# Two token tiles of the first MLP's second slice group computed together by seven block products

## The chip, the cores and the metric

The kernel runs on one core of one Trainium2 chip. The metric is the time of one execution on the device in microseconds (us); the kernel before has a median of 665.19 us over three runs (664.45, 665.19, 665.57).

## The reference

Three layers follow each other, all in float32. The first is a decaying linear attention over 2 batches, 8 heads and 768 positions with 64 channels. Its output becomes 1536 tokens of 512 channels. The second (MoE 1 in the code) and the third (MoE 2) are gated MLPs:

```python
# attention, per 64-position block (the kernel uses 128-position chunks)
intra = (q @ k.T * Dmask) @ v
inter = (q * lam_pow) @ kv_state
kv_state = lam_block * kv_state + (k * rev_pow).T @ v

# MoE 1: 1536 tokens, d_model 512, d_ff 1536
xn = x / sqrt(mean(x * x, -1) + 1e-6) * rms_g
g = xn @ w_gate
x = (g * sigmoid(g) * (xn @ w_val)) @ w_out

# MoE 2: the same shapes, no norm
out = ((x @ w_a) * (x @ w_b)) @ w_out
```

## The kernel before, in words

**Precision.** TensorE multiplies operands that are split into a high and a low part, and a product of two split matrices takes three matmuls: high by high, high by low, low by high. ScalarE makes the high part by a copy into a shorter format (`hi`, `uh`, line 292), VectorE subtracts it to get the low part (`lo`, `ul`, line 297). Weights come from memory as 64-bit numbers: ScalarE takes them apart in two copies (word `c`, lines 245 and 249), and VectorE puts a float32 together in seven operations (`k`, lines 266 to 280).

**Tiling.** The 1536 tokens are three tiles of 512 (0, 1, 2). The 1536 hidden columns are 12 slices of 128, in two groups (0 to 5, 6 to 11), and a slice's weights are three pieces of 128x512: gate, value, output. One *step* is one slice for one tile: 12 matmuls of 512 columns into a gate bank (`G`), 12 into a value bank (`V`), ScalarE's silu (`si`), VectorE's product with the value (`mu`), the split of the result (`hh`, `hl`), and 12 matmuls with the output weights into the four accumulator banks acc0 to acc3 (`O`). After a group the accumulators are copied or added into `sums` (`E`). Each tile splits the weights anew.

**Pairs.** In MoE 2 tiles 1 and 2 go together, by a scheme of seven block products in place of eight. The two tiles, each cut in two along the contraction, are the four blocks of one operand (B11, B21, B12, B22), gate and value of a slice those of the other. VectorE forms four sums of weight blocks (`ws`), the blocks' differences T1 to T4 are made once (`td`, `th`, `tl`), and seven products of 6 matmuls (`P`) go to three banks, with ScalarE's snapshots between them (`ps`) and VectorE's sums (`pa`). A product, a split and output matmuls follow as in a step (`pm`, `ph`, `pl`, `Q`). Since there are only four accumulator banks, tile 2's output matmuls wait until tile 1's are summed.

**Order.** Nothing is scheduled by a rule: the string PROGRAM lists every operation as a word (`G.12` is the gate of step 12), and each engine executes its words in that order. The queues of the engines are in order; a word waits for the data, buffers and PSUM banks that it needs. In MoE 1 before, steps run slice group by slice group, tile by tile: steps 18 to 23 are slices 6 to 11 for tile 0, 24 to 29 for tile 1, 30 to 35 for tile 2. Step 12 is the first after attention has ended.

**Norm.** For chunk c and batch b, ScalarE squares the attention output (`sq`), VectorE adds four column blocks in one reduction (`rd`, line 424), TensorE adds over partitions by a matmul with ones (`R`), VectorE adds epsilon (`ms`), GpSimd takes the power (`rr`), VectorE builds a diagonal (`dg`), TensorE spreads it (`N`), and VectorE scales four blocks (`nx`) before the split (`xh`, `xl`). `W` words are bf16 matmuls whose result nobody reads.

**Homes.** A converted weight slice lives in one of 8 slots of 128x1536; `third_of` puts the output piece of slice i into the slot of slice i+1.

Of the kernel before, what the change touches and what calls it, by code (L numbers as in the profile page):

```python
# [7 lines left out]
F32 = mybir.dt.float32  # L8
# [32 lines left out]
SLOTS = 8  # L41
# [7 lines left out]
    A.0.0.0 W.14 W.7.1 S.0.0 A.0.0.2 l.0 g Z A.1.0.0 A.1.0.2 D.0 A.0.1.0 D.1 l.1 A.1.1.3 A.1.1.0 A.1.1.2 c.0.1  # L49
    S.1.0 A.0.1.2 l.2 A.0.1.3 k.0.0.1 k.0.4.1 k.0.2.1 k.0.1.1 k.0.3.1 k.0.5.1 am.0.0.0 k.0.6.1 am.0.0.1 am.1.0.1  # L50
    am.1.0.0 kd.0.0 kd.1.0 X.0.0 U.0.0 hi.0.0 sq.0.0 xg.0.0 X.1.0 U.1.0 lo.0.0 l.3 L.0.2 sa.0.0 rd.0.0 sa.1.0
    qd.0.1 I.0.1 S.0.1 sq.1.0 c.0.2 xg.1.0 c.1.0 rd.1.0 am.0.1.1 S.1.1 am.0.1.0 k.0.0.2 k.0.4.2 am.1.1.0 R.0 ms.0
    am.1.1.1 qd.1.1 X.0.1 sq.0.1 l.4 W.8.1 I.1.1 X.1.1 sd.0.1 k.0.1.2 k.0.3.2 k.0.2.2 k.0.5.2 kd.1.1 rr.0 dg.0
    k.0.6.2 l.5 N.0 U.1.1 c.1.1 hi.0.1 xg.0.1 L.1.2 rd.0.1 sd.1.1 kd.0.1 nx.0.1 nx.0.3 nx.0.0 sq.1.1 lo.0.1 sa.1.1
    rd.1.1 nx.0.2 qd.0.2 U.0.1 xh.0.0 c.1.2 xh.0.1 xg.1.1 kd.0.2 R.1 ms.1 rr.1 xl.0.0 sa.0.1 k.1.0 xl.0.1 k.1.1
    dg.1 k.1.4 N.1 nx.1.3 nx.1.0 nx.1.1 nx.1.2 c.2.0 xh.1.0 k.1.3 xl.1.0 xh.1.1 k.1.5 xl.1.1 k.1.2 S.0.2 am.0.2.1
    am.0.2.0 l.9 l.7 l.6 kd.1.2 qd.1.2 c.2.2 c.2.1 G.0 l.8 I.0.2 X.0.2 U.0.2 si.0 sq.0.2 xg.0.2 L.0.3 sd.0.2 l.10
    k.2.0 k.1.6 rd.0.2 k.2.4 k.2.2 k.2.1 sa.0.2 k.2.3 V.0 hi.1.0 hi.0.2 c.3.0 hi.1.1 c.3.2 c.3.1 S.1.2 lo.1.0
    k.2.5 am.1.2.0 lo.0.2 mu.0 G.1 am.1.2.1 l.11 qd.0.3 U.1.2 I.1.2 X.1.2 sd.1.2 kd.0.3 l.13 l.12 k.3.0 lo.1.1
    k.2.6 hh.0 si.1 sq.1.2 rd.1.2 hi.2.0 sa.1.2 lo.2.0 k.3.2 k.3.1 k.3.4 k.3.3 V.1 R.2 ms.2 c.4.2 hi.1.2 hl.0 O.0  # L60
# [743 lines left out]
```

## Time and profile before

| | |
|---|---|
| median of 3 runs | 665.19 us |
| the profiled execution | 664.28 us, of which the span of its instructions 662.6 us |
| TensorE at work | 97% of the span |
| VectorE at work | 74% |
| ScalarE at work | 59% |
| GpSimd at work | 6% |
| mean granted TensorE clock | 0.987 |
| read from memory | 51.1 MB |

Times inside the span count from its first instruction. "Busy" counts a stretch in which several instructions overlap once. TensorE's instructions overlap (the next starts before the one ahead has ended), so a matmul's length in a row is not what it costs in a sequence; the distance from one start to the next is. The chain of work that ended last cuts such overlaps off, so its pieces add up.

### The profile page before, as it was taken

The numbers are of one execution on the slowest core, as the hardware profiler recorded it, in microseconds if no ns is written. First come the engines' busy times: TensorE is split into PE (matmuls) and PEld (weight loads), VectorE is DVE, ScalarE is ACT, GpSimd is POOL, SyncE is SP. The second block draws the span as 40 slices with busy tenths as digits, with TensorE's granted clock in tenths as the row PEclk, the third lists the DMA queues.
The fourth block names the chain that finished last, engine by engine and source line by source line (L and its number), as shares of the span: only waits on it lengthen the run. The fifth ranks groups of instructions, "written<-read, shape, count | busy, mean of one in ns | idle before, by whom it ended". The sixth has DMA issues, their size and how long they took to land.

```text
span 662.6 us, 8558 instructions
## 1 busy us (share of the span) xinstructions
PE 640.3 (97%) x3300; PEld 520.4 (79%) x3301; DVE 490.0 (74%) x781; ACT 389.1 (59%) x610; POOL 42.2 (6%) x43
## 2 busy tenths in 40 slices
PE   6869999999999999999999999999999999999997
PEld 4657787777888888888888888888887888888876
DVE  4789999865663878567357999887784797766583
ACT  2758777333578684364387974755648953444431
POOL 2523231210000000000000000000000000000000
PEclk9969999999999999999999999999999999999999
DMA  8946454110033331030033430201102400100011
GB/s 273 377 129 226 153 193 160 64 64 1 1 96 124 100 101 58 1 95 1 1 125 124 127 101 1 95 1 63 33 0 69 154 1 1 63 1 0 1 63 64
DMA packets 16505, 54.83 MB, mean 83 GB/s; under 512 B 1864, under 2 KB 3408, under 8 KB 15440
## 3 DMA queue, kind: packets, MB, share of 16 engines
q1 hardware_dynamic: 15600, 47.99, 22.0%
q10 hardware_dynamic: 864, 6.29, 2.7%
q8 instruction: 26, 0.43, 0.3%
q14 instruction: 15, 0.12, 0.1%
HBM read 51.12 MB, written 3.15 MB: 82 GB/s over the span
## 4 chain that ended last, share of the span: by engine, by line
PE 89%; DVE 8%; DMA 1%; issue 1%; ACT 0%; POOL 0%; DVEq 0%; POOLq 0%; ACTq 0%; SPq 0%
PE acc L534 29%; PE at L645 10%; PE gv L486 8%; PE gv L645 7%; PE gv L490 7%; PE gv L487 7%; PE at L490 5%; PE at L486 5%; PE at L487 5%; PE at L338 1%; PE at L388 1%; PE at L373 1%; DVE nrm L445 1%; DVE wlo L297 1%; DVE sums L546 1%; PE acc L388 1%
## 5 line engine op out<-in xcount | busy, mean ns | idle before, releaser
L297 DVE TENSOR_TENSOR wlo<-w,whi 128x512 fp32r<-128x512 f32 (+1 forms) x192 | 124.1, 674 | 10.2 <-ACT whi L292 10.0
L292 ACT CAST whi<-w 128x512 fp32r<-128x512 f32 (+1 forms) x192 | 108.9, 607 | 13.4 <-DVE w L278 7.0
L486 PE MATMUL gv<-xhi,whi 128*128 128x512 f32 x240 | 96.5, 402 | 0.3 <-DVE s L505 0.3
L487 PE MATMUL gv<-xlo,whi 128*128 128x512 f32 x240 | 94.4, 393 | 0.0
L245 ACT COPY hh<-stage 128x1024 uint8<-128x1024 uint8 x72 | 75.2, 1044 | 8.6 <-DMA stage<-w_dram 6.8
L509 ACT CAST hhi<-s 128x512 fp32r<-128x512 f32 x48 | 29.8, 621 | 78.9 <-DVE s L505 78.9
L249 ACT COPY w<-stage 128x1024 uint16<-128x1024 uint16 x72 | 75.4, 1047 | 0.0
L490 PE MATMUL gv<-xhi,wlo 128*128 128x512 f32 x240 | 64.5, 390 | 1.1 <-DVE wlo L297 1.0
L513 DVE TENSOR_TENSOR hlo<-s,hhi 128x512 fp32r<-128x512 f32 x48 | 34.6, 721 | 30.5 <-ACT hhi L509 30.4
L486 PE MATMUL at<-xhi,whi 128*128 128x512 f32 x144 | 56.0, 389 | 0.0
L487 PE MATMUL at<-xlo,whi 128*128 128x512 f32 x144 | 56.0, 389 | 0.0
L486 PEld LDWEIGHTS gv<-xhi,whi 128*128 128x128 f32 x240 | 45.6, 190 | 11.5 <-issue 0.9
L490 PEld LDWEIGHTS gv<-xhi,wlo 128*128 128x128 f32 x240 | 44.9, 188 | 11.3 <-DVE wlo L297 1.9
L487 PEld LDWEIGHTS gv<-xlo,whi 128*128 128x128 f32 x240 | 45.7, 190 | 9.1
L534 PE MATMUL acc<-whi,hlo 128*128 128x512 f32 x144 | 43.0, 391 | 0.0
L278 DVE SCALAR_TENSOR_TENSOR w<-w,hh 128x1536 f32<-128x1536 uint32 (+1 forms) x26 | 42.4, 1630 | 0.4
L534 PE MATMUL acc<-hhi,whi 128*128 128x512 f32 x144 | 42.1, 394 | 0.4 <-ACT hhi L509 0.4
L534 PE MATMUL acc<-hlo,whi 128*128 128x512 f32 x144 | 41.7, 391 | 0.9 <-DVE hlo L513 0.9
L534 PE MATMUL acc<-whi,hhi 128*128 128x512 f32 x144 | 42.2, 392 | 0.1
L534 PE MATMUL acc<-wlo,hhi 128*128 128x512 f32 x144 | 41.8, 389 | 0.0
L534 PE MATMUL acc<-hhi,wlo 128*128 128x512 f32 x144 | 41.5, 389 | 0.0
L505 DVE TENSOR_TENSOR s<-s,gv 128x512 f32<-128x512 f32 x30 | 20.5, 683 | 27.3 <-PE gv L490 27.2
(144 smaller groups left out, 1138.7 us busy)
## 6 DMA issues: line engine op xcount, KB each, us to landing
stage<-w_dram SPq DMA_DIRECT2D x72, 512.0 KB, 3.5
att<-att_dram ACTq DMA_DIRECT2D x6, 1024.0 KB, 4.8
att<-att_dram SPq DMA_DIRECT2D x6, 512.0 KB, 5.9
out_dram<-sums SPq DMA_DIRECT2D x12, 256.0 KB, 2.1
att<-att_dram SPq DMA_DIRECT2D x2, 1024.0 KB
att<-att_dram SPq DMA_DIRECT2D x4, 256.0 KB, 7.9
dt<-ext_d SPq DMA_DIRECT2D x2, 256.0 KB, 4.7
p<-ext_d SPq DMA_DIRECT2D x2, 128.0 KB, 6.3
```

The lines of the kernel that those rows point to most:

```text
L245: nc.scalar.copy(hh_t[i][:, into].bitcast(U8).rearrange("p (n e) -> p n e", e=2), st.rearrange("p (n e) -> p n e", e=8)[:, :, 3:5],)
L249: nc.scalar.copy(wres[i][:, into].bitcast(U16).rearrange("p (n e) -> p n e", e=2), st.bitcast(U16).rearrange("p (n e) -> p n e", e=4)[:, : ...
L278: nc.vector.scalar_tensor_tensor(out=w, in0=w32, scalar=2.0**-28, in1=hh.bitcast(BF16), op0=ALU.mult, op1=ALU.mult)
L292: nc.scalar.copy(whi[key], src)
L297: nc.vector.tensor_sub(wlo[key], src, whi[key].bitcast(F32))
L486: nc.tensor.matmul(ps, lhsT=w, rhs=xhi[t][:, k, :], start=k == 0, stop=False)
L487: nc.tensor.matmul(ps, lhsT=w, rhs=xlo[t][:, k, :], start=False, stop=False)
L490: nc.tensor.matmul(ps, lhsT=w, rhs=xhi[t][:, k, :], start=False, stop=k == KD - 1)
L509: nc.scalar.copy(h_t[g][0], s_t[g])
L513: nc.vector.tensor_sub(h_t[g][1], s_t[g], h_t[g][0].bitcast(F32))
L534: nc.tensor.matmul(acc[j], lhsT=lhsT, rhs=rhs, start=first and n == 0, stop=last and n == 2)
L645: nc.tensor.matmul(ps, lhsT=w[:, k * 128 : (k + 1) * 128], rhs=x[:, k, :], start=first and n == 0, stop=n == len(todo) - 1, skip_group_che ...
```

## The change

In MoE 1, slices 6 to 11 are computed for tiles 1 and 2 together by the seven block products that MoE 2 had already. Steps 18 to 23 (tile 0) stay; steps 24 to 35 of before go, and six paired slices take their place. For these, the blocks' differences are formed from the high and low parts that lie in SBUF (`tq`), and then split (`tH`, `tL`); ScalarE's silu is applied to the finished gate (`sl`).

Output pieces get homes of their own: 7 slots of 128x1024 for gate and value, 10 of 128x512 for output pieces. Two of the seven conversion operations (numbers 2 and 6) become two instructions each, one for each home.

In the norm of chunks 0 and 1 the reduction on VectorE goes: four matmuls add the squares' four blocks up in PSUM. Mean and epsilon go by batch. PROGRAM is written anew from start to end, with 46 matmuls of `W` in place of 29.

```diff
-SLOTS = 8
+SLOTS, OUT_SLOTS = 7, 10
...
-    A.0.0.0 W.14 W.7.1 S.0.0 A.0.0.2 l.0 g Z A.1.0.0 A.1.0.2 D.0 A.0.1.0 D.1 l.1 A.1.1.3 A.1.1.0 A.1.1.2 c.0.1
+    A.0.0.0 W.8.1 W.14 W.3.1 W.7.1 W.2.1 S.0.0 W.3.1 A.0.0.2 l.0 g Z A.1.0.0 A.1.0.2 D.0 D.1 A.0.1.0 A.1.1.3
...
+    def home(i, some):
+        if some.start == 0:
+            if i - 1 not in wout:
+                wout[i - 1] = wpool.tile([128, 512], F32, tag=f"o{(i - 1) % OUT_SLOTS}", name=f"o{i - 1}")
+            return wout[i - 1]
+        if i not in wres:
+            wres[i] = wpool.tile([128, 1024], F32, tag=f"w{i % SLOTS}", name=f"w{i}")
+        return wres[i][:, (some.start - 1) * 512 : (some.stop - 1) * 512]
...
+        if op in (2, 6):
+            for some in (slice(0, 1), slice(1, 3)) if place is None else (slice(place, place + 1),):
+                w = home(i, some)
+                hh = hh_t[i][:, some.start * 512 : some.stop * 512]
...
-    def mean_square(c):
-        ms_t[c] = ps = bank("at0")
-        for b in range(B):
-            nc.tensor.matmul(ps[:, b : b + 1], lhsT=sqs_t[b, c], rhs=ones[:, 0:1], start=True, stop=True)
+    def mean_square(b, c):
+        ms_t[b, c] = att_bank(b, c)
+        todo = [sqs_t[b, c]] if (b, c) in sqs_t else [sq_t[b, c][:, a * C : (a + 1) * C] for a in range(NP)]
+        for n, x in enumerate(todo):
+            nc.tensor.matmul(
+                ms_t[b, c][:, 0:1], lhsT=x, rhs=ones[:, 0:1], start=n == 0, stop=n == len(todo) - 1
+            )
...
-        for m in range(2) for lo, hi in GROUPS for t in range(1 if m else len(TILES)) for f in range(lo, hi)
+        for m in range(2) for lo, hi in GROUPS for t in range(1 if m or lo else len(TILES)) for f in range(lo, hi)
...
+    DIFFS = {
+        3: (("B12h", "B11h"), ("B12l", 1), ("B11l", -1)), 4: (("B22h", "T1"), ("B22l", 1)),
+        5: (("B22h", "B12h"), ("B22l", 1), ("B12l", -1)), 6: (("B21h", "T2"), ("B21l", 1)),
+    }
...
+    def part_diff(n, s):
...
+        if s == 0:
+            nc.vector.tensor_sub(o, of(a), of(b))
+        elif b == 1:
+            nc.vector.tensor_add(o, o, of(a))
+        else:
+            nc.vector.tensor_sub(o, o, of(a))
+
+    def diff_hi(n, k):
+        nc.scalar.copy(block(BLOCKS[n])[0][:, k, :], diff_home(n)[:, k, :])
+
+    def diff_lo(n, k):
+        hi, lo = block(BLOCKS[n])
+        nc.vector.tensor_sub(lo[:, k, :], diff_home(n)[:, k, :], hi[:, k, :].bitcast(F32))
...
+    def pair_silu(i, t):
+        nc.scalar.activation(s_t[i, t], s_t[i, t], AF.Silu)
```

Three places show how the instructions move. Lines 486, 487, 490 and 534 of before are 514, 515, 518 and 562 now.

TensorE, MoE 1, slice 6 for tile 1, before: the gate bank gv0 is filled by 12 matmuls from tile 1's parts (xhi1, xlo1), then the value bank.

```order
L486 MATMUL gv0_2522<-xhi1_778,whi_2482 128x512
L487 MATMUL gv0_2522<-xlo1_779,whi_2482 128x512
L486 MATMUL gv0_2522<-xhi1_778,whi_2482 128x512
L487 MATMUL gv0_2522<-xlo1_779,whi_2482 128x512
L490 MATMUL gv0_2522<-xhi1_778,wlo_2484 128x512 x4
L486 MATMUL gv1_2559<-xhi1_778,whi_2486 128x512
```

The same engine now, at slice 6 for tiles 1 and 2, from the end of tile 0's last output matmuls on: products 7, 4 and 3 of the slice (T3 is a difference block, xhi2 and xlo2 hold tile 2 or a difference).

```order
L562 MATMUL acc3_2405<-hlo_2622,whi_2588 128x512
L706 MATMUL gv0_2636<-T3_2489,whi_2643 128x512 x4
L706 MATMUL gv0_2636<-T3_2489,wlo_2645 128x512 x2
L706 MATMUL gv0_2636<-xhi2_1480,whi_2656 128x512
L706 MATMUL gv0_2636<-xlo2_1481,whi_2656 128x512
L706 MATMUL gv0_2636<-xhi2_1480,whi_2656 128x512
L706 MATMUL gv0_2636<-xlo2_1481,whi_2656 128x512
L706 MATMUL gv0_2636<-xhi2_1480,wlo_2662 128x512 x2
L706 MATMUL at0_2664<-xhi2_1480,whi_2643 128x512
```

Products of 6 matmuls stand where steps of 36 stood, and product 4 follows product 7 into the same bank with nothing between; ScalarE's snapshot of product 7 has to read that bank first.

VectorE in the paired slices now, around slices 9 and 10 (wsum are sums of weight blocks, h2 and s are gates and products of tiles 2 and 1, o12 and w13 are homes of MoE 2's weights).

```order
L727 TENSOR_TENSOR h2_2802<-h2_2802,usum_2351 128x512
L675 TENSOR_TENSOR wsum_2221<-w9_1973 128x256
L675 TENSOR_TENSOR wsum_2221<-w9_1973,wsum_2221 128x256
L301 TENSOR_TENSOR hh_2710<-hh_2710,t_2824 128x1536
L727 TENSOR_TENSOR s_2819<-s_2819,gv1_2840 128x512
L317 TENSOR_TENSOR wlo_2903<-o8_1980,whi_2891 128x512
L286 SCALAR_TENSOR_TENSOR o12_2760<-o12_2760,hh_2710 128x512
L286 SCALAR_TENSOR_TENSOR w13_2712<-w13_2712,hh_2710 128x1024
L317 TENSOR_TENSOR wlo_2931<-w9_1973,whi_2900 128x512
```

Sums, splits and pair products of MoE 1 and the conversion of MoE 2's weights (lines 301 and 286) share the queue; before, tile 1's and tile 2's steps stood there.

VectorE in the norm of the first chunk, before (line 424 is the reduction, am a masked score, wlo a weight's low part).

```order
L349 TENSOR_TENSOR am<-gv_176,dt 128x512
L297 TENSOR_TENSOR wlo<-w_172,whi 128x512
L424 TENSOR_REDUCE nrm<-sq 128x128 x2
L349 TENSOR_TENSOR am<-at_268,dt 128x512
L349 TENSOR_TENSOR am<-at_267,dt 128x512
L266 TENSOR_SCALAR t<-hh 128x512
```

The same place now (line 461 adds epsilon, for one batch; lines 349, 297 and 266 are 369, 317 and 293 now).

```order
L369 TENSOR_TENSOR am<-gv_200,dt 128x512
L286 SCALAR_TENSOR_TENSOR w_197<-w_197,hh 128x512
L461 TENSOR_SCALAR ms<-acc_282 128x1
L369 TENSOR_TENSOR am<-at_258,dt 128x512
L369 TENSOR_TENSOR am<-at_259,dt 128x512
L317 TENSOR_TENSOR wlo<-w_197,whi 128x512
L293 TENSOR_SCALAR t<-hh 128x512
```

The two reductions are gone from this place, two more from a later one, and the epsilon of batch 0, which waits for TensorE, stands ahead of the next chunk's masks.

## Rows read from the trace of the kernel before

**Rows 1.** The page: span, busy time and share by engine.

```profile
span 662.6 us, 8558 instructions
PE 640.3 (97%) x3300; PEld 520.4 (79%) x3301; DVE 490.0 (74%) x781; ACT 389.1 (59%) x610; POOL 42.2 (6%) x43
```

**Rows 2.** Busy time by stretch: length, then each engine's, clock, DMA share, GB/s.

```profile
0.00:42.50 42.50, 28.48 (x285) 20.97 (x286) 28.91 (x64) 22.40 (x32) 16.56 (x23) 0.83 0.80 279
42.50:113.40 70.90, 67.72 (x477) 53.29 (x476) 67.23 (x98) 54.11 (x77) 17.99 (x14) 0.98 0.53 179
278.60:376.50 97.90, 97.90 (x434) 81.09 (x433) 64.55 (x98) 63.47 (x96) 0.00 (x0) 1.00 0.23 72
376.50:425.60 49.10, 49.10 (x218) 40.69 (x217) 46.54 (x70) 32.98 (x52) 0.00 (x0) 1.00 0.22 73
425.60:518.10 92.50, 92.50 (x404) 75.35 (x404) 70.25 (x118) 59.25 (x100) 0.00 (x0) 1.00 0.14 43
```

**Rows 3.** The chain that ended last, by time: start, length, what; steps, then pairs.

```profile
243.36 2.72 PE acc L534 x12
251.52 2.72 PE acc L534 x12
...
458.94 1.36 PE gv L645 x6
460.30 0.68 PE acc L534 x3
460.98 1.65 PE gv L645 x6
```

**Rows 4.** VectorE's groups by form: count, busy us, mean ns, idle before and releasers.

```profile
L297 DVE TENSOR_TENSOR wlo<-w,whi 128x512 fp32r<-128x512 f32 x180 | 119.3, 691 | 10.2 <-ACT whi L292 10.0
L278 DVE SCALAR_TENSOR_TENSOR w<-w,hh 128x1536 f32<-128x1536 uint32 x23 | 40.3, 1753 | 0.4
L278 DVE SCALAR_TENSOR_TENSOR w<-w,hh 128x512 f32<-128x512 uint32 x3 | 2.1, 686 | 0.0
L424 DVE TENSOR_REDUCE nrm<-sq 128x128 f32<-128x512 f32 x12 | 12.9, 1078 | 9.9 <-ACT sq L420 9.9
L276 DVE TENSOR_TENSOR hh<-hh,t 128x1536 uint16<-128x1536 uint16 x23 | 22.0, 955 | 0.4
L268 DVE TENSOR_SCALAR t<-t 128x1536 uint16<-128x1536 uint16 x23 | 13.8, 602 | 0.4
L614 DVE TENSOR_TENSOR wsum<-wsum,w 128x256 f32<-128x256 f32 x12 | 5.1, 424 | 0.3
L604 DVE TENSOR_TENSOR sums<-sums,sums 128x1024 f32<-128x1024 f32 x3 | 3.7, 1218 | 0.0
```

**Rows 5.** VectorE's instructions in order of time, at 35, 42 and 400 us.

```profile
35.45 1.61 DVE L268 TENSOR_SCALAR t<-t 128x1536 uint16<-128x1536 uint16 x1
42.22 0.69 DVE L470 TENSOR_TENSOR xlo<-spare,xhi 128x512 fp32r<-128x512 f32 x1
399.77 1.89 DVE L297 TENSOR_TENSOR wlo<-w,whi 128x512 fp32r<-128x512 f32 x3
```

**Rows 6.** GpSimd's instruction beside the slow one of VectorE at 35 us.

```profile
34.94 1.71 POOL L329 TENSOR_TENSOR spare<-att,p 128x512 f32<-128x512 f32 x1
```

**Rows 7.** The chain at the first step's gate.

```profile
42.55 0.72 PE gv L486
43.27 0.43 PE gv L487
...
46.85 1.02 PE at L373 x16
47.87 1.05 PE at L388 x16
```

More of the change, by code (lines that the diff above doesn't have):

```diff
@@ L162 @@
+    uh.19.5 ul.19.5 ph.19.2 pl.19.2 Q.18.2.0.12 ph.20.2 uh.20.5 ul.20.5 pl.20.2 Q.19.2.0.12 uh.22.5 uh.21.5
+    ul.21.5 ph.21.2 pl.21.2 Q.20.2.0.12 ul.22.5 ph.22.2 pl.22.2 Q.21.2.0.12 uh.23.5 ul.23.5 ph.23.2 pl.23.2
+    Q.22.2.0.12 Q.23.2.0.12 e.23.2.0 e.23.2.1 e.23.2.2 e.23.2.3
 """.split()
@@ L228, in load_w @@
         stage[n] = t
-    wres, hh_t, t_t = {}, {}, {}
-    def third_of(i, part):
-        return (i + 1, 0) if part == 2 else (i, part + 1)
+    wres, wout, hh_t, t_t = {}, {}, {}, {}
+    def home(i, some):
[6 more added lines that the diff above has]
+        return wres[i][:, (some.start - 1) * 512 : (some.stop - 1) * 512]
     def conv_copy(i, place):
-        if i not in wres:
-            wres[i] = wpool.tile([128, 1536], F32, tag=f"w{i % SLOTS}", name=f"w{i}")
+        if i not in hh_t:
             hh_t[i] = vpool.tile([128, 1536], U16, tag="hh", name="hh")
@@ L249, in conv_copy @@
         nc.scalar.copy(
-            wres[i][:, into].bitcast(U16).rearrange("p (n e) -> p n e", e=2),
+            home(i, slice(place, place + 1)).bitcast(U16).rearrange("p (n e) -> p n e", e=2),
             st.bitcast(U16).rearrange("p (n e) -> p n e", e=4)[:, :, 0:2],
@@ L258, in conv_op @@
             place = 0
-        some = slice(0, 1536) if place is None else slice(place * 512, (place + 1) * 512)
         if i not in t_t and op != 2:
             t_t[i] = vpool.tile([128, 1536], U16, tag="t", name="t", bufs=1)
-        hh, w = hh_t[i][:, some], wres[i][:, some]
-        t = t_t[i][:, some] if op != 2 else None
-        w32 = w.bitcast(U32)
+        if op in (2, 6):
+            for some in (slice(0, 1), slice(1, 3)) if place is None else (slice(place, place + 1),):
+                w = home(i, some)
+                hh = hh_t[i][:, some.start * 512 : some.stop * 512]
+                w32 = w.bitcast(U32)
+                if op == 2:
+                    nc.vector.tensor_scalar(
+                        w32, w32, 0x0FFFFFFF, 0x10000000, op0=ALU.bitwise_and, op1=ALU.bitwise_or
+                    )
+                else:
+                    nc.vector.scalar_tensor_tensor(
+                        out=w, in0=w32, scalar=2.0**-28, in1=hh.bitcast(BF16), op0=ALU.mult, op1=ALU.mult
+                    )
+            return
+        some = slice(0, 1536) if place is None else slice(place * 512, (place + 1) * 512)
+        hh, t = hh_t[i][:, some], t_t[i][:, some]
         if op == 0:
@@ L274, in conv_op @@
             nc.vector.tensor_scalar(hh, hh, 0x8000, None, op0=ALU.bitwise_and)
-        elif op == 5:
+        else:
             nc.vector.tensor_tensor(out=hh, in0=hh, in1=t, op=ALU.bitwise_or)
-        else:
-            nc.vector.scalar_tensor_tensor(
-                out=w, in0=w32, scalar=2.0**-28, in1=hh.bitcast(BF16), op0=ALU.mult, op1=ALU.mult
-            )
     whi, wlo = {}, {}
     def third(i, part):
-        i, place = third_of(i, part)
-        return wres[i][:, place * 512 : (place + 1) * 512]
+        return wout[i] if part == 2 else wres[i][:, part * 512 : (part + 1) * 512]
     def unit_hi(key, src):
```

255 lines of the change are left out of this document (138 added, 117 removed).

## The prediction

> **What bounds the kernel now.** The page comes first: TensorE is at work for 97% of the span, VectorE for 74% [rows 1]. A mean over stages says little, so the stretches come next [rows 2]. From 278.6 to 518.1 us TensorE is busy every microsecond at the full clock; VectorE's share goes from 66% (64.55 of 97.90, plain steps) over 95% (46.54 of 49.10, where MoE 2's tile differences are made) to 76% (70.25 of 92.50, MoE 2's pairs). From 42.5 to 113.4 us it is the other way round: VectorE fills 67.23 of 70.90 us, and TensorE has gaps. The chain of waits gives the price of TensorE's work: output matmuls start at 243.36 and again at 251.52 us, so a step of 36 matmuls takes 8.16 us, 0.227 each, with nothing waited for [rows 3]. A matmul removed after step 12 is worth 0.227 us, as long as VectorE and ScalarE keep up.
>
> **Products: −8.16 us.** A slice for tiles 1 and 2 took two steps of 36 matmuls; it takes 7 products of 6 and 24 output matmuls, 66. Six slices drop 36 matmuls: 36 × 0.227 = 8.16 us.
>
> A rule speaks against that price. The Trainium skill ("Perfetto Trace Analysis", Identifying the Most-Contended Engine) says that matmul busy time shows badly how near TensorE is to its limit, and that the busy share of weight loads shows it better. That share is 79% here [rows 1]; an estimate by the rule would count 36 × 0.227 × 0.79 = 6.5 us. The distance of 0.227 us from start to start over a stretch without a wait speaks for the full price.
>
> **VectorE in the paired slices: +2 us, between 0 and 21.** What an instruction costs in a queue is the distance between starts: three splits of 0.69 us took 1.89 together [rows 5], so each costs 0.60, or 0.08 to 0.09 less than its length. Between the first product of slice 6 and step 24, VectorE's queue holds 96 sums, splits and products of the paired slices: 70 of 512 columns at 0.60 and 26 of 256 at 0.42 − 0.08 = 0.34 [rows 4], 51 us. It holds the conversion of five slices of MoE 2. Each has four 16-bit operations at 0.60 − 0.08, one at 0.95 − 0.08 [rows 4], a third operation at some 0.95, and the seventh, now in two parts of 0.69 and, half way to the 1.75 of 1536 columns, 1.22 [rows 4], less 0.17: 5.6 us, for five slices 28. And it holds 21 sums and splits of neighbouring stages at 0.60, 13 us. Together 92 us, where TensorE has 6 × 66 + 12 matmuls, 92.5 us. So VectorE has nothing to spare, and each gap of its queue that the conversions don't fill is TensorE's. The nearest rows: at 376.5 to 425.6 VectorE was 95% busy and TensorE waited for nothing, which is the lower end, 0. In MoE 2's six paired slices VectorE lay idle for 92.50 − 70.25 = 22.25 us [rows 2]; all of that beside 92 us of work would take 114 us, 21 more than TensorE's work. I take 2, one of them for one place: in slice 6 product 4 follows product 7 into the same bank. In MoE 2, where 3 matmuls (0.68 us) stood between such two, product 4 took 1.65 us in place of 6 × 0.227 = 1.36 [rows 3], so ScalarE's snapshot and its signals need 0.68 + 0.29 = 0.97 us, which nothing hides now. For the rest I stay near the lower end, 1 us: a low part is needed only by the last 2 of a product's 6 matmuls and the last 4 of the 12 of a gate or an output, and conversions can fill waits here as they did at 376.5.
>
> **Differences, homes: 0, between 0 and 4.** In steps 12 to 23 VectorE gets 12 × 5 instructions at 0.60 (36), six slices' conversions (34), ten differences of 1024 columns at 1.22 − 0.08 [rows 4] and eight splits (16): 86 us, where TensorE has 97.9. The steps at 278.6 show no gap at 66% of VectorE, the row after it none at 95% [rows 2]; this is 88%. Were the differences not covered by the 12 us to spare, 16 − 12 = 4 us would show. It can't come out below nothing, since a step without a wait can't be shorter than 8.16.
>
> **The start: −2.4 us, between −5.7 and +2.** The first step's gate begins at 42.55 us [rows 7] and waits for the last split of chunk 1, 42.22 to 42.91 [rows 5]. Ahead of that split VectorE's queue loses four reductions (1.08 − 0.08 each [rows 4], 4.0) and gains one conversion's third operation (0.95), two masks (1.20) and two small ones (0.15): 1.7 us shorter. I let the gate begin 1.6 us sooner, if waits and delays stay. Three groups of attention matmuls (1.02 and 1.05 [rows 7], and some 0.65 for half as wide ones) now stand ahead of that gate, where TensorE would be idle; so 2.7 us less comes after it. Against this stands VectorE's queue after the gate: up to the low part for step 2's output it has 27 conversion operations (21 us), 24 instructions at 0.60 (15), two reductions (2) and some small ones (2.4), 40.4 us. TensorE has 35.8 us up to that output, and 1.8 more before it needs the low part. That is a wait of 2.8 us; in before's order the worst place has 1.6 − 1.8, none. And the clock: the gate's first matmuls were 0.43 us apart [rows 7], at 1.2 of 2.4 GHz; the mean clock of 0.98 over 70.90 us [rows 2] makes it 1.4 us lost. Seventeen more warm-up matmuls may keep it; I count 0.9. Sum: −1.6 − 2.7 + 2.8 − 0.9 = −2.4. At the lower end the wait is covered and the clock full, −1.6 − 2.7 − 1.4 = −5.7. At the upper end the gate is late: SyncE's queue has two weight loads, where it had one, ahead of the last of chunk 1's values, 512 KB at 279 GB/s [rows 2], 1.9 us; 1.9 − 2.7 + 2.8 = +2.
>
> **The sum.** The profiled execution took 664.28 us, its span 662.6 and 1.7 around it; −8.16 + 2 + 0 − 2.4 = −8.6 makes 655.7. The median of the runs lies 0.9 above that execution, so I forecast 656.5 us.
>
> **Rivals.** *VectorE bounds the pairs (slower).* A product goes over ScalarE's snapshot, VectorE's sum, silu, VectorE's product, ScalarE's split and VectorE's low part back to TensorE; these chains may keep the idle time that MoE 2's pairs show. For it: VectorE's load equals TensorE's. Against it: 95% without a wait at 376.5 [rows 2]. At full price 656.5 − 2 + 21 = 675.5; it decides, and the kernel is slower, once more than half of the 22 us is kept. Chance 8%.
>
> *VectorE is delayed beside GpSimd at the start.* The instruction of line 268 took 1.61 us at 35.45, where GpSimd worked from 34.94 to 36.65 [rows 5, 6]; its mean is 0.60 [rows 4]. Each such meeting costs 1.0 us, and five more make the start 5 us longer, since VectorE fills 95% of it: 661.5 us. For it: GpSimd's 16.56 us before 42.5 [rows 2] are the same instructions and meet another order. Against it: before has such meetings too, and as many may go. Chance 14%. The Trainium skill ("SBUF — State Buffer", Who interferes with whom) has it that the two engines share a pair of ports that one instruction holds to its end, and that a reduction never meets this lock. The row at 35.45 agrees with the first; by the second the four reductions that go were none of the delayed ones.
>
> *The start gives all.* −5.7 there and 0 for the pairs: 651.3 us. Chance 12%.
>
> *No change.* About half of the idle time kept: within 0.2%, which is about what a measurement of this kernel can tell from no change. Chance 5%.
>
> **How the numbers follow.** The forecast, with a range of its own of 653 to 660, has 61%. Faster by over 0.2% is the forecast, the delayed start and the best start, 87%; the same 5%, slower 8%. The range for 8 in 10 leaves out the last two cases, a fifth of the delayed start and a third of the best start: 650.5 to 662.5.
>
> **What would show it.** Right: steps still 8.16 us apart from step 12 on; the paired slices of MoE 1 within 3 us of 92.5 with VectorE above 93%; one gap of about 1 us at slice 6, between two products into the same bank; step 12 near 178 us. Wrong: products or output matmuls that wait for VectorE's low parts in several paired slices (the first rival); slow instructions of VectorE beside GpSimd's and a late step 12 (the second); steps 12 to 23 together longer than 98 us (the differences that I set to 0).

## The result, and the profile after

The kernel before took 664.84 us in the median of its runs, the changed kernel 656.66 us: ratio 0.9881, 95% interval [0.9847, 0.9915]. A second set gave 663.89 and 657.44 us, 0.9895 [0.988, 0.9911]. The forecast was 656.5 us. The profiled executions took 664.28 and 655.50 us, 8.78 less, where the sum of the terms said 8.6. That execution of the changed kernel is the fastest of its four, and another profiled one, the yardstick below, took 658.67 us; so how near the sum came hangs in part on which execution was profiled. Single executions of the changed kernel lie between 655.5 and 659.3 us; part of what makes that spread is told below.

The page of the changed kernel, span and busy time by engine, against [rows 1]:

```profile
span 653.8 us, 8719 instructions
PE 638.9 (98%) x3304; PEld 517.5 (79%) x3306; DVE 520.1 (80%) x889; ACT 405.0 (62%) x642; POOL 39.7 (6%) x43
```

The windows of the changed kernel, cut where its stages begin: length, then busy time of TensorE, its weight loads, VectorE, ScalarE and GpSimd, granted clock, DMA share, GB/s. They answer to [rows 2]. In order: up to the first gate, from there to step 2's output, steps 12 to 23, the paired slices of MoE 1, steps 24 up to the first pair of MoE 2, and the rest.

```profile
0.00:44.40 44.40, 38.52 (x372) 27.17 (x374) 29.11 (x68) 25.36 (x34) 17.98 (x24) 0.88 0.82 286
44.40:83.70 39.30, 37.29 (x259) 29.90 (x257) 37.34 (x66) 32.82 (x46) 8.90 (x8) 1.00 0.58 193
...
177.88:275.80 97.92, 97.92 (x433) 81.08 (x432) 86.95 (x134) 72.71 (x111) 0.00 (x0) 1.00 0.30 97
275.80:370.38 94.58, 93.50 (x410) 76.26 (x408) 89.36 (x158) 79.94 (x126) 0.00 (x0) 1.00 0.27 85
370.38:416.62 46.24, 46.24 (x206) 38.29 (x204) 41.01 (x66) 24.93 (x44) 0.00 (x0) 1.00 0.10 32
416.62:649.60 232.98, 232.89 (x1021) 190.71 (x1019) 169.33 (x294) 129.91 (x217) 0.00 (x0) 1.00 0.12 39
```

The first matmuls of the stages, counted off in both traces, give the account. Step 12 begins at 180.64 us before and at 177.88 now: 2.76 less. Steps 12 to 23 take 97.92 us in both. From there to MoE 2's first product it was 425.44 − 278.56 = 146.88 us and is 416.62 − 275.80 = 140.82: 6.06 less, which is 8.16 for 36 matmuls less 2.10 for waits. The rest takes 233.0 us in both.

What TensorE waited for in the paired slices, from the view of waits of the changed kernel, 275 to 372 us (engine, line, what it waited for, us, times, longest; waits under 0.15 us are not in this view, and there is one, of 0.09 us):

```profile
PE gv L706 <- ACT usum L721: 0.7, 1, 0.7
PE acc L562 <- DVE hlo L741: 0.3, 1, 0.3
```

The chain of waits of the changed kernel shows the first of them, between products 7 and 4 of slice 6, and, in the second piece, the end of tile 1. The first two rows are the outputs of two steps, which answer to [rows 3].

```profile
265.09 2.72 PE acc L562 x12
...
273.25 2.72 PE acc L562 x12
...
284.13 1.37 PE gv L706 x6
285.50 0.02 issue
285.52 0.59 ACT usum L721
286.12 0.04 issue
286.16 1.66 PE gv L706 x6
```
```profile
350.49 0.69 DVE hlo L741
...
353.86 0.70 DVE sums L574
354.56 0.04 issue
354.60 3.47 PE acc L562 x14
```

Output matmuls still start 8.16 us apart. In MoE 2, 0.68 us of output matmuls stood between products 7 and 4 [rows 3]; here nothing does, TensorE stands still while ScalarE copies the bank, and its next matmuls start slowly: 0.95 us in all. At the end of tile 1 its last output waits for a low part (0.67 with the slow starts), and tile 2's first output for the banks that VectorE adds up (0.37). All but 0.1 us of the rest of these 94.58 us is 408 matmuls at 0.2267.

The start reads differently from what was forecast. The chain of the changed kernel from the spread of chunk 1's scale factors (L478) over chunk 2's scores (L358) and its three attention groups (L378 keys with values, L393 the state, L408 the masked scores with values) to the first gate, against [rows 7]; and the same spread and scores (L338) in the kernel before:

```profile
34.62 1.24 PE at L478 x4
...
37.69 1.67 PE at L358 x12
...
40.21 1.12 PE at L378 x16
41.33 1.90 PE at L393 x16
43.24 1.24 PE at L408 x16
44.47 0.43 PE gv L514
```
```profile
37.41 0.77 PE at L450 x2
...
40.51 2.04 PE at L338 x14
```

The spread came 2.79 us sooner, the end of the scores 3.19 (39.36 against 42.55), and the gate 1.92 us later. In both kernels the gate begins right behind what stands ahead of it in TensorE's queue: the scores before, the groups now.

### The profile page after: what moved, and what is told of

Its sections match the earlier page's. It is cut to its first block, busy times and chain, and to the rows that moved or that the text cites. A ratio compares the mean times of both kernels' runs of the same rounds, so it can differ in the third digit from the quotient of the medians.

```text
span 653.8 us, 8719 instructions
## 1 busy us (share of the span) xinstructions
PE 638.9 (98%) x3304; PEld 517.5 (79%) x3306; DVE 520.1 (80%) x889; ACT 405.0 (62%) x642; POOL 39.7 (6%) x43
## 4 chain that ended last, share of the span: by engine, by line
PE 86%; DVE 9%; DMA 2%; SPq 1%; ACT 1%; issue 0%; POOL 0%; ACTq 0%; DVEq 0%; POOLq 0%
PE acc L562 27%; PE at L706 15%; PE gv L706 11%; PE gv L514 6%; PE gv L518 6%; PE gv L515 5%; PE at L515 3%; PE at L514 3%; PE at L518 3%; DMA att<-att_dram 1%; DVE sums L574 1%; PE at L393 1%; PE at L358 1%; DVE wlo L317 1%; PE at L408 1%; DVE hh L301 1%
## 5 line engine op out<-in xcount | busy, mean ns | idle before, releaser
L514 PE MATMUL gv<-xhi,whi 128*128 128x512 f32 x192 | 76.7, 399 | 0.0
L317 DVE TENSOR_TENSOR wlo<-w,whi 128x512 fp32r<-128x512 f32 (+1 forms) x108 | 69.7, 654 | 7.8 <-ACT whi L312 7.8
L515 PE MATMUL gv<-xlo,whi 128*128 128x512 f32 x192 | 74.9, 390 | 0.0
L312 ACT CAST whi<-w 128x512 fp32r<-128x512 f32 (+1 forms) x108 | 60.5, 585 | 14.1 <-PE acc L562 5.6
L317 DVE TENSOR_TENSOR wlo<-o,whi 128x512 fp32r<-128x512 f32 x72 | 50.5, 705 | 3.5 <-ACT whi L312 3.4
L264 ACT COPY w<-stage 128x1024 uint16<-128x1024 uint16 x48 | 50.2, 1045 | 0.0
L312 ACT CAST whi<-o 128x512 fp32r<-128x512 f32 x72 | 44.2, 620 | 8.9 <-PE acc L562 4.3
L562 PE MATMUL acc<-hlo,whi 128*128 128x512 f32 x144 | 42.1, 392 | 0.9 <-DVE hlo L541 0.6
L562 PE MATMUL acc<-whi,hlo 128*128 128x512 f32 x144 | 42.9, 391 | 0.0
L562 PE MATMUL acc<-hhi,whi 128*128 128x512 f32 x144 | 42.5, 395 | 0.2
L562 PE MATMUL acc<-whi,hhi 128*128 128x512 f32 x144 | 42.2, 392 | 0.1
L562 PE MATMUL acc<-wlo,hhi 128*128 128x512 f32 x144 | 41.8, 390 | 0.0
L562 PE MATMUL acc<-hhi,wlo 128*128 128x512 f32 x144 | 41.5, 390 | 0.0
L706 PE MATMUL at<-T,whi 128*128 128x512 f32 x144 | 38.5, 389 | 0.0
L514 PE MATMUL at<-xhi,whi 128*128 128x512 f32 x96 | 37.3, 389 | 0.0
L515 PE MATMUL at<-xlo,whi 128*128 128x512 f32 x96 | 37.3, 389 | 0.0
```

Of the source, the lines that this page charges most:

```text
L264: nc.scalar.copy(home(i, slice(place, place + 1)).bitcast(U16).rearrange("p (n e) -> p n e", e=2), st.bitcast(U16).rearrange("p (n e) -> p ...
L312: nc.scalar.copy(whi[key], src)
L317: nc.vector.tensor_sub(wlo[key], src, whi[key].bitcast(F32))
L514: nc.tensor.matmul(ps, lhsT=w, rhs=xhi[t][:, k, :], start=k == 0, stop=False)
L515: nc.tensor.matmul(ps, lhsT=w, rhs=xlo[t][:, k, :], start=False, stop=False)
L562: nc.tensor.matmul(acc[j], lhsT=lhsT, rhs=rhs, start=first and n == 0, stop=last and n == 2)
```

## Experiments

Times of a stage are those of one profiled execution; "behind the spread" is the distance from the spread of chunk 1's scale factors to step 12 (143.26 us with the changed kernel, 143.23 before), which takes out how early an execution's data came. In the diffs, numbers are those of the program's words; each engine executes its own words in this order. In the runs with product 3 moved, the reductions back and the gate ahead, a line that is L562 elsewhere is L557, and the others are five lower too.

The runs came in four sets on four chips: the first four, the next four, the two that follow, and the last two. Behind each median stands its ratio to the kernel before in the same set (663.89, 664.21, 664.67 and 665.09 us), with its 95% interval; across sets only the ratios compare well.

Six of the profiled executions have the same words up to step 12: the changed kernel's two, and the runs with product 3 moved, 36 matmuls less and the two with more work for VectorE. In them step 12 began at 177.53 to 181.07 us, 143.07 to 145.38 behind the spread. What a run changed at the start has to stand out from that.

**The yardstick.** The changed kernel again.

> The changed kernel as it is, beside the runs of the kernel before on the same chip: the yardstick for the experiments that follow. Every theory: 655.5 us for a profiled execution, 12 steps from 177.9 us on that take 97.9 us, and 94.6 us for the six paired slices of MoE 1 (2.1 above 408 x 0.2267), of which 0.95 stand between products 7 and 4 of slice 6, and 1.0 at tile 1's last output and the end of its sums.

657.44 us, 0.9895 [0.988, 0.9911]; the profiled execution was the slowest of its five, 658.67. Steps 12 to 23 took 97.92 us and the pairs 94.53, as in the first; all of the 3 us more lies ahead of step 12 (181.07), and 2.08 of it ahead of the spread (36.70). VectorE and GpSimd of this execution at 35 us, and of the first one:

```profile
35.45 2.21 DVE L473 TENSOR_SCALAR nrm<-ident,rr 128x128 f32<-128x128 f32 x2
```
```profile
35.30 1.27 POOL L349 TENSOR_TENSOR spare<-att,p 128x512 f32<-128x512 f32 x1
36.52 1.06 POOL L337 TENSOR_TENSOR spare<-att,dt 128x512 f32<-128x512 f32 x1
```
```profile
34.28 0.48 DVE L473 TENSOR_SCALAR nrm<-ident,rr 128x128 f32<-128x128 f32 x2
```
```profile
36.39 1.27 POOL L349 TENSOR_TENSOR spare<-att,p 128x512 f32<-128x512 f32 x1 [2.14 <-DMA att<-att_dram]
```

Where GpSimd is at work on chunk 2's values, two small instructions of VectorE on the chain take 2.21 us in place of 0.48. In two other runs (reductions back, fewer reductions) they took 2.21 and 2.33, with GpSimd at work beside them from the start; in the other ten executions, where GpSimd still waited for these values when they began, 0.48. Such meetings are not confined to this place: in the fourteen profiled executions 160 instructions of VectorE ahead of 180 us took over 0.15 us more than the median of their kind, and all 160 overlap one of GpSimd; none of the 20 reductions that overlap one was slow. Ahead of that pair, TensorE's granted clock was 0.83 between 20 and 30 us, where it had been 1.00.

**Product 3 between products 7 and 4.**

```
- P.6.7 ps.6.7 P.6.4 bh.0.2 uh.8.0 pa.6.2 pm.6.1 ph.6.1 P.6.3
+ P.6.7 ps.6.7 P.6.3 P.6.4 bh.0.2 uh.8.0 pa.6.2 pm.6.1 ph.6.1
```

> In slice 6 product 3 is issued between products 7 and 4 (it goes to another bank); nothing else moves. Theory A (product 4 waits only for ScalarE's snapshot of the bank that it shares with product 7, and VectorE keeps up with the pairs): the 0.95 us between the two products go, since 1.36 us of product 3 stand in their place; the paired slices take 93.6 instead of 94.6 us, 654.6 us in all. Theory B (VectorE's queue sets the length of the paired slices, and the wait for product 4 only hides a wait that would come later): the gap is gone there and comes back at products or outputs of slices 7 to 9; 94.6 us and 655.5 in all.

655.34 us, 0.9874 [0.9859, 0.9889]; the pairs took 94.17 us, 0.41 less. Neither theory in full. The wait at product 4 is gone; in its place stands one at product 4 of slice 7, which follows its product 7 by one product only:

```profile
PE acc L557 <- DVE hlo L736: 0.3, 1, 0.3
PE at L701 <- ACT usum L716: 0.3, 1, 0.3
```

TensorE is 0.95 us earlier there and ScalarE isn't: its snapshot for that product begins 22.94 us after the first product in both kernels. Ahead of it ScalarE waited for a sum of VectorE:

```profile
297.85 0.64 ACT L728 ACTIVATE h<-h 128x512 f32<-128x512 f32 x1 [0.28 <-DVE h L722]
```

So 0.55 of the 0.95 comes back, at slice 7, as theory B has it, and 0.41 is kept.

**The four reductions back.**

```
- R.0.0 ... R.1.0 ... R.0.1 ... R.1.1
+ rd.0.0 R.0.0 ... rd.1.0 R.1.0 ... rd.0.1 R.0.1 ... rd.1.1 R.1.1
```

> The four sums of squares of chunks 0 and 1 are made by VectorE's reductions again (four of 1.08 us, some 4.0 us in its queue), each followed by 1 matmul in place of 4. Theory A (VectorE's queue bounds the start up to step 2's output): step 12 begins 3 to 4 us later, at 181 to 182 us, and the whole takes 658.5 to 659.5. Theory B (the start is set by when TensorE can begin and by its clock, and a longer queue on VectorE is absorbed by waits it has anyway): step 12 within 0.7 us of 177.9, 655 to 656.2 in all.

661.18 us, 0.9958 [0.9945, 0.9971]: 3.7 us slower than the yardstick. By its size this is theory A, by its place not. The reduction stands in the chain that ends at the spread, which comes at 40.25 us; behind the spread there are 144.59 us, as in the yardstick (144.37). In both of these executions the two small instructions met GpSimd, so 3.55 us between their spreads (40.25 and 36.70) is like against like. The chain of this run:

```profile
36.23 0.96 DVE nrm L439
37.19 0.14 issue
37.32 0.37 PE acc L449 x2
```

**The gate ahead of chunk 2's groups.**

```
- k.1.5 am.0.2.0 am.0.2.1 xl.1.1 k.1.2 xl.1.0 l.7 c.2.2 k.1.6 U.0.2 I.0.2 X.0.2 G.0
+ k.1.5 xl.1.1 xl.1.0 am.0.2.0 am.0.2.1 k.1.2 l.7 c.2.2 k.1.6 G.0 U.0.2 I.0.2 X.0.2
```

> The two low parts of chunk 1's values that the first gate needs go ahead of the masks of chunk 2 on VectorE, and the three groups of chunk 2's attention matmuls go behind the first gate on TensorE, as they stand in the kernel before. The gate then begins some 4 to 5 us sooner, at 39.5 to 40.5 instead of 44.4 us. Theory A (VectorE's queue bounds the start, and a sooner gate is waited away at step 2's output): step 12 between 177.0 and 178.2 us, 654.6 to 655.8 in all. Theory B (as the terms of the prediction add up: the gate's start counts in full, less the 2.6 us of the groups that come after it): step 12 near 175.8, 653.4 in all.

659.71 us, 0.9937 [0.9923, 0.9951]: slower, against both theories. The gate began at 39.06 us, 5.34 sooner than in the first execution of the changed kernel, and step 12 at 181.17, 3.29 later and 146.87 behind the spread. VectorE stood idle ahead of chunk 2's reduction (the time in brackets):

```profile
48.87 1.04 DVE L439 TENSOR_REDUCE nrm<-sq 128x128 f32<-128x512 f32 x1 [5.12 <-ACT sq L435]
```

**Fewer reductions.** The words rd.0.2, rd.1.2, rd.0.3 and rd.1.3 go.

> The reductions of chunks 2 and 3 go as well (four of some 1.05 us on VectorE); their sums of squares are made by 4 matmuls each on TensorE, as those of chunks 0 and 1. Theory A (VectorE's queue alone bounds the start): step 12 begins 2 to 4 us sooner than with the changed kernel in the same state (177.9 to 181.1 us), 652 to 654.5 in all. Theory C (formed from the run with the early gate, where VectorE stood idle for 5.1 us ahead of the reduction of chunk 2 and the whole became 2.3 us longer: what counts is when VectorE's next instruction gets its operand; the reductions are where it waits for TensorE's attention groups): the idle time ahead of those reductions, 1.1 and 0.7 us, goes with them, so the gain is 4 us of work and up to 1.8 of waits: step 12 at 173 to 175.5, 650 to 653 in all. Theory B (TensorE sets the start): 0 to +1 us, since TensorE gets 12 small matmuls more.

659.40 us, 0.9937 [0.9925, 0.995]: 2 us slower than the yardstick (2.8 by the ratios), with 4 us less work on VectorE. Theories A and C of the start fall; theory B said +1 at most. The spread came at 36.25; VectorE met GpSimd there as in the yardstick (2.33 us for the two small instructions), and the groups and the gate's first matmuls behind it ran at half speed (1.90 us where 1.02 is full speed). But step 12 is 146.80 behind the spread, and 2.3 of the 3.5 us more than in the first execution of the changed kernel lie behind the groups. Of these 0.6 is the gate (3.49 us for 2.87, since its first matmuls were slow) and 0.7 the sum of squares, whose eight matmuls took 0.80 us where two took 0.14; what the other 1.0 is stays open.

**36 matmuls less.** In the last six pairs of MoE 2 the matmuls with the weights' low part are left out of products 1, 3 and 6.

```
+ todo = todo[:4] if i >= 18 and n in (1, 3, 6) else todo
```

> In the last six paired slices of MoE 2 the two matmuls with the weights' low part are left out of products 1, 3 and 6: 36 matmuls of 128x512 less, and nothing else is changed (VectorE makes the low parts as before). Theory A (a matmul is worth its distance from start to start, 0.227 us): the stage from step 30 to the end is 8.2 us shorter, 131.2 instead of 139.4. Theory B (the busy share of weight loads, 79%, says how near TensorE is to its limit, as the Trainium skill's rule in Perfetto Trace Analysis, Identifying the Most-Contended Engine, has it): 6.5 us shorter. Theory D (VectorE and ScalarE are late once TensorE has less to do there): under 6 us, with gaps at products.

647.64 us, 0.9768 [0.9743, 0.9794]. The windows from step 30 to the end, of this run and of the changed kernel:

```profile
510.32:641.76 131.44, 131.36 (x576) 107.53 (x575) 96.79 (x168) 68.02 (x116) 0.00 (x0) 1.00 0.10 33
```
```profile
510.18:649.56 139.38, 139.29 (x613) 114.45 (x611) 97.29 (x168) 68.53 (x116) 0.00 (x0) 1.00 0.09 31
```

7.94 us less, 0.221 a matmul: theory A within 0.2 us. The estimate by the rule of the Trainium skill (Perfetto Trace Analysis, Identifying the Most-Contended Engine) was 6.5 us; the measurement decides for the distance from start to start.

**6.8 us more for VectorE in the pairs.** Each word ws.7.1 to ws.11.4 stands twice.

> Each of the 20 weight sums of slices 7 to 11 of MoE 1 is made twice, one behind the other: 20 x 0.34 = 6.8 us more for VectorE, spread over the paired slices, with the same results. Theory A (as the prediction: VectorE has nothing to spare there, 89.4 us busy of 94.6): the paired slices take 96.5 to 100 us, since at best the idle 5.2 us take up the work, and they stand where they can't be used. Theory B (the two places where TensorE waits are the whole of it, and VectorE runs ahead elsewhere): 94.6 to 95.5.

662.65 us, 0.9971 [0.9957, 0.9986]; the pairs took 99.50 us, 4.92 more: theory A. TensorE's waits in them:

```profile
PE acc L562 <- DVE hlo L741: 2.2, 2, 1.9
PE at L706 <- ACT usum L721: 1.9, 1, 1.9
PE gv L706 <- ACT usum L721: 0.7, 1, 0.7
```

Of 6.8 us, 1.9 found room. The room is small, and the waits appear at two new places (1.95 and 1.93 us, and 0.12 at a third), not as a delay of every product.

**6.7 us more for VectorE in steps 12 to 23.** The words k.7.4 to k.12.4 stand three times, k.8.1 and k.10.1 twice.

> Fourteen conversion instructions of slices 7 to 12 are made twice (the mask of the sign three times in each slice, two clampings twice): 14 x 0.48 = 6.7 us more for VectorE in steps 12 to 23, with the same results. Theory A (VectorE has 11 us to spare there, 87.0 us busy of 97.9, and they can be used): steps 12 to 23 still take 97.9 us, and the whole is as long as without. Theory B (VectorE's idle time there lies where its operands are missing and can't be used): 1 to 5 us longer.

660.17 us, 0.9941 [0.9917, 0.9964]; these steps took 101.63 us, 3.71 more: within what theory B said, but only 2.04 of it is VectorE's lateness (a wait of 1.76 us and the slow matmul behind it). The other 1.67 is a stretch behind it at a lower clock:

```profile
PE acc L562 <- DVE hlo L541: 1.8, 1, 1.8
```
```profile
229.60:235.00 5.40, 5.40 (x18) 4.29 (x17) 5.30 (x11) 3.16 (x5) 0.00 (x0) 0.68 0.02 3
```

The mean of 11 us to spare hides a stretch without any: the changed kernel's windows of a quarter of these steps each.

```profile
177.88:202.40 24.52, 24.52 (x110) 20.30 (x109) 18.82 (x32) 23.65 (x36) 0.00 (x0) 1.00 0.40 129
202.40:226.84 24.44, 24.44 (x109) 20.24 (x108) 23.47 (x39) 21.85 (x29) 0.00 (x0) 1.00 0.61 193
```

VectorE is busy for 23.47 of 24.44 us in the second, and the wait came at its end, 47.9 us behind the start of step 12.

**Warm-ups in the gaps.**

```
+ W.3.1 R.1.1 ... W.7.1 N.1 ... W.5.1 S.0.2 ... W.2.1 U.0.2
```

> Seventeen warm-up matmuls more, in TensorE's gaps between 30.9 and 40.2 us (3 ahead of the second sum of squares of chunk 1, 7 ahead of the spread of its scale factors, 5 and 2 ahead of chunk 2's scores and state); nothing else moves. Theory K (the clock that falls in those gaps is what the start loses: granted clock 0.50 from 34 to 42 us, so chunk 2's attention groups took 4.3 us for 2.6 and the gate's start came late): the gate begins 1 to 2 us sooner after the spread (9.8 us behind it with the changed kernel, 8 to 9 now), step 12 comes 1 to 2 us sooner for the same start of the spread, 653.5 to 655.5 in all. Theory A (VectorE's queue bounds the start): step 12 stays 143.3 us behind the spread, 655.5 to 657.5 in all. Theory L (the warm-ups stand in the way): later by up to 2 us.

655.01 us, 0.9862 [0.9842, 0.9883]; the gate began 7.57 us behind the spread (9.78 in the first execution of the changed kernel), step 12 141.87: theory K. That is 1.4 us less than the first execution of the changed kernel and 1.2 below the lowest of the six with its start; the totals alone don't tell it from the yardstick, since the intervals meet. The clock from 34 to 42 us, of this run and of the changed kernel:

```profile
34.00:38.00 4.00, 3.28 (x23) 1.83 (x23) 3.93 (x10) 2.93 (x5) 2.56 (x3) 1.00 0.74 224
38.00:42.00 4.00, 3.54 (x58) 2.72 (x56) 4.00 (x7) 3.71 (x4) 0.64 (x2) 1.00 0.44 131
```
```profile
34.00:38.00 4.00, 2.26 (x8) 1.77 (x10) 3.75 (x10) 2.66 (x4) 1.86 (x3) 0.50 0.71 236
38.00:42.00 4.00, 3.52 (x38) 3.13 (x38) 3.10 (x6) 3.90 (x5) 1.40 (x1) 0.50 0.30 92
```

**The early gate, with work for VectorE.**

```
- G.0 U.0.2 I.0.2 X.0.2 xg.0.2 sq.0.2 hi.6.2 rd.0.2 hi.1.1 lo.1.1 k.2.0 hi.1.0 lo.1.0 k.2.4 R.0.2
+ G.0 hi.1.1 lo.1.1 k.2.0 hi.1.0 lo.1.0 k.2.4 U.0.2 I.0.2 X.0.2 xg.0.2 sq.0.2 hi.6.2 rd.0.2 R.0.2
```

The lines marked − are those of the run with the early gate.

> As the run with the early gate, and VectorE and ScalarE get the splits of slice 1's first two weights and two conversion instructions ahead of the values of chunk 2, so that VectorE isn't idle for 5.1 us ahead of the reduction of chunk 2. Theory C (with the early gate the loss was VectorE without an operand): the loss goes, step 12 at or below 143.3 us behind the spread of chunk 1's scale factors (146.9 with the early gate alone), 654 to 656.5 in all. Theory K (the early gate lost by the clock: a gate and three groups at half speed): step 12 stays some 146 us behind the spread, 658 to 660 in all.

660.40 us, 0.9932 [0.9914, 0.9951]; step 12 147.16 behind the spread. Theory C falls: VectorE has work and nothing is gained. Theory K's numbers come nearest (146 said), and the granted clock was 0.50 from 34 to 42 us. But the clock is not the whole: TensorE stands for 2.35 us ahead of the sum of squares, behind the groups, as it did in the run with the early gate:

```profile
49.64 0.35 PE L454 MATMUL at<-ones,nrm 128*128 128x1 f32 x2 [2.35 <-DVE nrm L444]
```

**Both gains.** Product 3's place and the warm-ups together.

> The two changes that gained alone, together: product 3 between products 7 and 4 in slice 6, and the seventeen warm-up matmuls in the start's gaps. If they are independent: the paired slices 93.6 to 94.2 us, step 12 141.9 us behind the spread of chunk 1's scale factors, 653.3 to 654.5 us in all. If the one takes the other's gain (TensorE earlier, so that VectorE is late at slice 7): 654.5 to 655.5.

653.80 us, 0.9828 [0.9809, 0.9848], the fastest of all that leave no work out: its interval lies below that of the yardstick and meets that of the first set only at its edge. Step 12 141.06 behind the spread; the pairs 94.17 us, as with product 3's place alone. Both numbers are as for independent gains.

**Both, with the early gate.** As the run before this, with the early gate, and R.0.2 behind V.0. Three more words moved that the expectation doesn't name: the two warm-ups of W.2.1 are gone, hi.1.0 stands ahead of lo.1.1, and rd.0.2 behind lo.1.1, k.2.0, lo.1.0 and k.2.4.

> As the run with both, with the first gate ahead of chunk 2's attention groups again, and with the sum of squares' matmul of chunk 2 behind the first value instead of ahead of it. Theory R (formed from the fed early gate, whose TensorE stood for 2.35 us at that matmul, waiting for square and reduction behind the groups: the gate behind the groups is what covers this chain, and the value can cover it as well): no gap over 0.5 us between the groups and the second gate, and step 12 no later behind the spread than with both, 141.0 to 142.0 us; 652.5 to 654.5 in all. Theory A (VectorE's queue bounds it once the clock is full): the same, with gaps at step 2's output or before it. Theory K (only the clock matters, the early gate brings it down): step 12 at 143 or more behind the spread, with a granted clock below 0.9 from 38 to 46 us.

657.71 us, 0.9887 [0.9868, 0.9905]; step 12 147.06 behind the spread. Theory R falls. Both signs that theory K named are there (147.06, and a granted clock of 0.79 from 38 to 46 us), but they don't show that only the clock matters: a wait of 2.54 us stands at the same matmul as in the fed run, and VectorE waited 5.37 us ahead of a low part. Here are the two rows:

```profile
53.08 0.35 PE L454 MATMUL at<-ones,nrm 128*128 128x1 f32 x2 [2.54 <-DVE nrm L444]
```
```profile
49.75 0.69 DVE L317 TENSOR_TENSOR wlo<-w,whi 128x512 fp32r<-128x512 f32 x1 [5.37 <-ACT whi L312]
```

Since the reduction stands further back in this order too, the run doesn't test theory R alone.

**What the runs of the start have in common.** In 12 of the 13 executions of the changed kernel and its variants, step 12 begins 133.4 to 134.4 us after the end of the last group of chunk 2's attention (the one at L408 above), which lay between 41.9 and 51.4 us; the one apart is the run with fewer reductions, 135.7. The distance is the same whether the gate stands ahead of the groups or behind them:

| run | spread | groups end | step 12 | from groups' end |
|---|---|---|---|---|
| before | 37.41 | 48.90 | 180.64 | 131.74 |
| changed | 34.62 | 44.47 | 177.88 | 133.41 |
| changed, again | 36.70 | 46.93 | 181.07 | 134.14 |
| reductions back | 40.25 | 51.36 | 184.84 | 133.48 |
| gate first | 34.30 | 47.71 | 181.17 | 133.46 |
| gate first, fed | 34.49 | 47.30 | 181.65 | 134.36 |
| warm gaps | 34.66 | 42.30 | 176.53 | 134.23 |
| both gains | 34.49 | 41.92 | 175.56 | 133.63 |
| both, gate first | 34.48 | 47.56 | 181.53 | 133.98 |

So a gate ahead of these groups delays them and step 12 with them, and a gate behind them costs nothing more. But the mark is not the only one that fits. From the start of batch 1's last attention group of chunk 2 (the next group at L408, 56.93 us in the changed kernel and 58.81 before) to step 12 it is 120.8 to 121.9 us in all 14 executions, the kernel before and the run with fewer reductions included. The distances suggest that the start is decided ahead of these groups; which of the links there (batch 0's groups, squares, reduction, VectorE's queue) decides it was not separated.

## Why the prediction was right, point by point

**Products, −8.16: right.** Steps 8.16 us apart before and after, pairs of 66 matmuls at 0.2267 with nothing between but the waits named; the 36 matmuls taken out elsewhere gave 7.94.

**VectorE in the paired slices, +2: right, 2.10.** The one place named came as said: 0.97 forecast, 0.95 measured. The 1 us for the rest was 1.04, at a place that wasn't named (tile 1's end). The first rival, that VectorE bounds the pairs, didn't come: 94.58 us instead of 114. But the premise that VectorE has next to nothing to spare holds: 4.92 of 6.8 us added came through.

**Differences and homes, 0: right**, 97.92 us in both. The reason was wrong: the spare time was counted over all of the 97.9 us, 12 us; in the second quarter VectorE has 1 us, and 6.7 us added cost 3.71, of which 1.67 by the clock.

**The start, −2.4: right in its sum in the execution that was profiled (−2.76), by luck, and wrong in its steps.** In the six executions with this start step 12 came 3.11 us sooner to 0.43 later than in the one profiled execution of the kernel before. The step that failed is "I let the gate begin 1.6 us sooner", and with it that the groups moved ahead of the gate stand "where TensorE would be idle". The gate doesn't wait for the split that the prediction names: before, it began at 42.55 us, and that split ended only at 42.91 [rows 5, 7]. It begins at its turn in TensorE's queue. The scores ahead of it ended 3.19 us sooner, and in the run with the gate ahead of the groups it did begin at 39.06; but from the scores' end to the groups' end it took 5.11 us, the first mask and then the groups, 4.3 us where 2.7 is full speed, and so the gate began 1.92 us later. The wait of 2.8 us at step 2's output that was set against it was 0.4; a gate 3.5 us later than forecast leaves VectorE that much more time, which would account for it. Both errors hang on one thing, that the gate was taken for the start's path.

Counted along the groups instead: their end came 48.90 − 44.47 = 4.43 us sooner, and 1.67 of it came back behind them. Of the 4.43, 2.79 is the earlier spread. The sums of squares no longer wait in VectorE's queue (with the reductions back the spread came 3.55 later than in the yardstick); but the kernel before also had two slow instructions of VectorE beside GpSimd in the chain ahead of its spread, 1.55 us at 33.98 and the 1.61 of [rows 5], together 1.9 us more than their kinds take, so how much of the 2.79 is the reductions' is not shown. The other 1.64 lies between spread and groups' end, where the gate's 4.3 us [rows 7] no longer stand, and where the first mask, the keys-with-values group (behind the others before) and slower groups now do. The 1.67 is not simply the gate's new place: its 12 matmuls do stand behind the groups now, but with the gate ahead of them again the distance to step 12 is 133.46 and 134.36 us, no shorter than 133.41, and a wait stands there instead.

**The clock, −0.9: wrong in its place.** The gate's own matmuls are at full speed (0.23 us apart behind the first), but the groups ahead of it took over the slow stretch. Seventeen warm-ups more in the gaps ahead of them gave 1.4 us.

**VectorE beside GpSimd (14%): the rival's five meetings more didn't come.** Counted ahead of 180 us, the kernel before had 12 instructions of VectorE that were slow beside GpSimd, 9.4 us lost in all; the changed kernel had 10 and 7.6 us in its first execution, 13 and 9.9 us in the yardstick. In the first execution the two small instructions on the chain ran free, but a split behind the gate did not:

```profile
52.41 1.60 POOL L349 TENSOR_TENSOR qd<-att,p 128x512 f32<-128x512 f32 x1 [7.38 <-DMA att<-att_dram]
52.78 1.77 DVE L317 TENSOR_TENSOR wlo<-o,whi 128x512 fp32r<-128x512 f32 x1
```

In the yardstick, the run with the reductions back and the run with fewer reductions the small ones met it too, 1.7 to 1.9 us. That is part of why the changed kernel's executions differ by 3.8 us. The rows agree with what the Trainium skill says of the two engines' shared ports (SBUF — State Buffer, Who interferes with whom).

## What to carry to other kernels

When two waits of different signs are set against each other in a term, ask first which chain ends the stage: here four terms met the sum by luck, and the marks in the trace (spread, scores, groups) show where each of them went. Before an instruction is said to wait for another, compare the two times: the gate began 0.36 us ahead of the end of the split that it was said to wait for. A spare share of an engine is worth what it is in the stretch where the work lands, so cut the windows as fine as the stages, and don't average over twelve steps. A wait removed beside engines that are nearly full comes back in part at the next late copy: 0.41 of 0.95 us was kept. And one profiled execution is one sample: six with the same start differ by 3.5 us at step 12.

## What was not expected of the hardware

The granted clock fell in a stretch where TensorE waited once, for 1.76 us, behind 47 us of work without a gap: matmuls were then 0.43 us apart, and the clock was 0.68 over the 5.40 us that followed. It didn't fall after two waits of 1.95 and 1.93 us in the paired slices with more work on VectorE. The first wait cost 3.71 us, these two 2.2 each, so nearly the same wait can cost once or twice its length; what made the difference is not shown. And two instructions of VectorE with 128 columns, 0.48 us together, took 2.2 to 2.3 us beside GpSimd's in three executions, as part of a pattern without an exception here: ahead of 180 us VectorE was slow only where it overlaps GpSimd.
